# All instructions of an attention and FFN kernel issued in an order that the kernel works out itself

## The chip, the cores and the metric

The kernel runs on one NeuronCore of a Trainium2 chip. The metric is the device time of one execution in microseconds. Five engines run beside each other, each in the order of its own instruction queue: TensorE (PE; its weight loads are listed as PEld), VectorE (DVE), ScalarE (ACT), GpSimd (POOL) and SyncE (SP). SP does nothing here but start DMA transfers, one after another.

## What is computed

The reference is sliding-window attention with a linear bias, followed by a gated FFN. q, k and v have 8 batches, 8 heads, 576 positions and 64 dimensions; the FFN is 512 wide with an inner width of 2048, over 8 x 576 = 4608 rows. All is float32.

```python
scores = scale * np.matmul(q, k.transpose(0, 1, 3, 2))
mask = (rel >= 0) & (rel < 128)                 # rel = query position - key position
scores = np.where(mask, scores - slopes * rel, -1e9)
attn = softmax(scores)                          # slopes: 2 ** -(head + 1)
x = np.matmul(attn, v)                          # then (4608, 512)
h = x @ w_in
g = h * (1.0 / (1.0 + np.exp(-1.702 * h)))
out = g @ w_out
```

## The kernel before

**Number format.** For the large matmuls each float32 operand is split into a rounded high part (type fp32r) and a remainder, and the three products high x high, high x remainder, remainder x high are summed. The weights arrive as 64-bit words and are decoded on the chip: `decode` (L211) runs, for each half megabyte of weights, two ScalarE passes (L219, L220), two VectorE passes (L221, L222), a ScalarE copy that makes the high part (L224) and a GpSimd subtraction that makes the remainder (L225). There are 16 such pieces of w_in and 16 of w_out.

**FFN.** The 4608 rows are cut into 18 chunks of T = 256. A chunk takes 16 steps f. `up(f)` (L448) is twelve matmuls into the tile `h_ps`; then follow the gate, as a Tanh on ScalarE (L457) and a multiplication on VectorE (L458), and the split of g (L461 on ScalarE, L462 on GpSimd). `down(f)` (L465) is six matmuls into two accumulators. A step is thus 18 matmuls, and there are 288 steps. Chunk 0 is done in two parts: its first F0 = 8 steps, then all of chunk 1, then the other 8 of chunk 0. `split_x` (L432) makes the parts of a chunk's input x when the chunk begins.

**Attention.** The work is cut into units of one or two blocks of 128 queries. A unit goes through a software pipeline, one stage per `tick()` (L510): its loads (`load`, `load_v`), the split of q and k, `scores` into `s_ps` (L298), `biased` with the row minimum on VectorE (L314), `exponents` on ScalarE (L328), `normal` (L337), the transposes `flip` into `t_ps` (L351), the copies `high` and `low`, `mix` with v into `x_ps` (L385), and `sum_up`, which writes a part of a chunk's x. Batch 0 is cut into 24 "whole" units: its matmuls are in plain float32, each shown as two in the profile (L303, L393), and its `normal` runs on GpSimd (L345). The other batches use the split format (L309, L398). Chunk 0 can begin when the first 8 units are through.

**What sets the order.** The program is written as one list: an opening of ticks until the first 8 units are mixed, then the 288 steps, with ticks and decodes put between them at a pace worked out from due steps. The framework's own scheduler (`schedule_with_timeline_sim`) then reorders each engine's instructions by its own timeline. Two things are held in the written order: SP's transfers (`move`, L168) and the idle matmuls of `spin` (L193), which keep TensorE busy while it has nothing else: 32 at the start (FIRST_SPINS) and 3 after each tick of the opening. In the opening, weight pair f is fetched four ticks late (`fetch_upto(ticks - FETCH_TICK)`), and the first two decodes are written at ticks 5 and 6.

Tiles come from pools with a number of rotating buffers; a new tile waits until the buffer's last reader is done. `rq` and `rk`, the raw q and k of a unit, have three each, and the table that `tables()` (L177) builds the bias from, `rel`, borrows one of the buffers of `rq`.

Of the kernel before, what the change touches and what calls it, by code (L numbers as in the profile page):

```python
# [21 lines left out]
P = 128  # L22
# [14 lines left out]
BESIDE = range(8, 24)  # L37
FETCH_TICK = 4
DECODE_TICK = 5
# [4 lines left out]
FIRST_SPINS = 32  # L44
SPINS = 3
# [110 lines left out]

@with_exitstack
def tile_kernel(ctx: ExitStack, tc: tile.TileContext, qT, kT, v, w_in, w_out, out):
# [3 lines left out]
    raw = ctx.enter_context(tc.tile_pool(name="raw", bufs=3))  # L162
    att = ctx.enter_context(tc.tile_pool(name="att", bufs=2))
    xp = ctx.enter_context(tc.tile_pool(name="xp", bufs=1))
    ffn = ctx.enter_context(tc.tile_pool(name="ffn", bufs=2))
    ps = ctx.enter_context(tc.tile_pool(name="ps", bufs=1, space=PSUM))

    def move(dst, src):  # L168

        tc.keep_in_program_order(nc.sync.dma_start(dst, src))  # L170
# [6 lines left out]
    def tables():  # L177
# [14 lines left out]

    def spin(n):  # L193

        m = ident.bitcast(BF16)
        for _ in range(n):
            tc.keep_in_program_order(nc.tensor.matmul(idle[:, :2 * P], m[:, :P], m, start=True, stop=True))  # L197
# [4 lines left out]
    def fetch(src, name):  # L202
        st = const.tile([P, 512], I64, name="r" + name, tag=name)
        move(st, src)
        return st
# [5 lines left out]
    def decode(st, name):  # L211

        words = st.bitcast(I32).rearrange("p (m two) -> p m two", two=2)
        top, low = words[..., 1], words[..., 0]
        part = st.bitcast(U16).rearrange("p (m four) -> p m four", four=4)[..., 1]
        bits = ps.tile([P, 4 * P], F32, name="w_ps", tag="t_ps", bufs=2).bitcast(I32)
        w = ffn.tile([P, 512], F32, name="wc", tag="o", bufs=3)

        nc.scalar.activation(bits.bitcast(F32), top.bitcast(F32), AF.Copy, scale=2.0 ** -112)  # L219
        nc.scalar.activation(low, part, AF.Copy, bias=2.0 ** -14 - 0.5, scale=2.0 ** -13)  # L220
        nc.vector.scalar_tensor_tensor(bits, bits, 3, low, ALU.logical_shift_left, ALU.bitwise_or)  # L221
        nc.vector.scalar_tensor_tensor(w.bitcast(I32), top, -0x80000000, bits, ALU.bitwise_and, ALU.bitwise_or)  # L222
        res = const.tile([P, 2, 512], F32R, name=name, tag=name)
        nc.scalar.copy(res[:, 0], w)  # L224
        nc.gpsimd.tensor_tensor(res[:, 1], w, res[:, 0].bitcast(F32), ALU.subtract)  # L225
        return res
# [15 lines left out]
    def load(u):  # L242
# [4 lines left out]
        u.rq = raw.tile([P, 2 * P], F32, name="rq", tag="rq")  # L247
        u.rk = raw.tile([P, 3 * P], F32, name="rk", tag="rk")
        rows = D if u.whole else P
        move(u.rq[:rows, :u.nq], qT[u.pair, :rows, u.q0:u.q0 + u.nq])  # L250
        move(u.rk[:rows, :u.nk], kT[u.pair, :rows, u.k0:u.k0 + u.nk])

    def load_v(u):
        if u.whole:
            u.rv = att.tile([P, 3, D], F32, name="VV", bufs=3)
        else:
            u.rv = raw.tile([P, 3, D], F32, name="rv", bufs=2)
# [3 lines left out]
        if full:  # L261
            move(u.rv[:, :full], v[u.pair, v0:v0 + full * P, :].rearrange("(c p) d -> p c d", p=P))
            u.spans.append((P, slice(0, full)))
        if full < len(u.loaded):
            m = u.loaded[-1].n
            move(u.rv[:m, full], v[u.pair, v0 + full * P:v0 + full * P + m, :])
            u.spans.append((m, slice(full, full + 1)))
        if u.whole:
            for i, c in enumerate(u.loaded):
                c.v = u.rv[:c.n, i]  # L270

    def split_q(u):
# [388 lines left out]
```

## Time and profile before

| | |
|---|---|
| median of 3 runs | 1069.94 us (1067.32 to 1072.7) |
| the profiled execution | 1072.22 us, of which its span is 1070.4 us |
| TensorE matmul, busy | 1054.6 us |
| TensorE weight loads, busy | 941.6 us |
| VectorE / ScalarE / GpSimd, busy | 706.7 / 605.4 / 636.1 us |
| moved by DMA | 81.24 MB, 76 GB/s in the mean |
| mean granted TensorE clock | 0.993 |

The span is the time from the first to the last instruction; the time of the execution is 1.8 us longer. Matmuls overlap in the array, so the duration of one (some 280 ns for 256 columns) is longer than the distance to the next, and a TensorE that is shown as busy need not be at its pace. Its pace is read from the number of matmuls in a stretch, or from the chain of work, where consecutive matmuls stand with the time that they took together.

### The profile page before, as it was taken

How to read it: one execution, taken by the hardware profiler on the slowest of the kernel's cores; microseconds unless marked ns; L12 is line 12 of the kernel's file. 1: busy time of each engine (PE TensorE's matmuls, PEld its weight loads, DVE VectorE, ACT ScalarE, POOL GpSimd, SP SyncE). 2: the span in 40 equal slices, each digit the busy share in tenths (PEclk: the TensorE clock that was granted, in tenths of full speed). 3: DMA queues.
4: the chain of work that ended last, by engine and by line, in shares of the span. 5: the costliest groups of instructions: out<-in, count | busy, mean ns of one | idle time of the engine just before them, and what ended most of it. 6: DMA issues, size and time to landing. Idle time of an engine off the chain costs nothing.

```text
span 1070.4 us, 21794 instructions
## 1 busy us (share of the span) xinstructions
PE 1054.6 (99%) x7021; PEld 941.6 (88%) x7021; DVE 706.7 (66%) x2299; ACT 605.4 (57%) x1797; POOL 636.1 (59%) x931
## 2 busy tenths in 40 slices
PE   7999999999999999999999999999999999999998
PEld 4676899998989999999999999999999999998987
DVE  4767898879897777654676668767867687413131
ACT  4797776676766566444555556656565556322222
POOL 3679986667776666544565657656666566323232
PEclk9799999999999999999999999999999999999999
DMA  4974322333322232202222212222222121000000
GB/s 136 305 235 145 83 63 86 105 84 86 86 79 80 60 88 77 61 12 67 63 71 66 62 52 86 72 69 67 85 67 85 52 68 51 9 12 21 1 21 20
DMA packets 97265, 81.24 MB, mean 76 GB/s; under 512 B 50048, under 2 KB 88448, under 8 KB 97152
## 3 DMA queue, kind: packets, MB, share of 16 engines
q1 hardware_dynamic: 91968, 70.42, 23.4%
q10 hardware_dynamic: 5184, 9.44, 2.4%
q8 instruction: 55, 0.90, 0.3%
q14 instruction: 58, 0.48, 0.1%
HBM read 70.39 MB, written 9.44 MB: 75 GB/s over the span
## 4 chain that ended last, share of the span: by engine, by line
PE 93%; DVE 3%; ACT 2%; DMA 1%; issue 1%; POOL 0%; SPq 0%; DVEq 0%; POOLq 0%; ACTq 0%
PE h_ps L452 37%; PE acc L471 37%; PE x_ps L398 5%; PE t_ps L364 5%; PE s_ps L309 5%; PE s_ps L303 1%; PE x_ps L393 1%; PE acc L197 1%; DMA rk<-kT 1%; DMA rw<-w_in 1%; DVE pb L321 1%; ACT pb L332 0%; ACT rw L220 0%; DVE xh L436 0%; SPq L170 0%
## 5 line engine op out<-in xcount | busy, mean ns | idle before, releaser
L452 PE MATMUL h_ps<-xh,w 128*128 128x256 f32 x2304 | 370.1, 284 | 3.6 <-DVE g L458 2.1
L462 POOL TENSOR_TENSOR gl<-g,gh 128x256 fp32r<-128x256 f32 x288 | 215.7, 750 | 255.8 <-ACT gh L461 194.4
L452 PEld LDWEIGHTS h_ps<-xh,w 128*128 128x128 f32 x2304 | 328.2, 188 | 34.7 <-DVE g L458 3.4
L471 PE MATMUL acc<-w,gh 128*128 128x512 f32 x1152 | 325.5, 399 | 0.0
L458 DVE SCALAR_TENSOR_TENSOR g<-g,h_ps 128x256 f32<-128x256 f32 x288 | 119.4, 415 | 180.5 <-ACT g L457 178.9
L457 ACT ACTIVATE g<-h_ps 128x256 f32<-128x256 f32 x288 | 109.6, 381 | 204.1 <-PE h_ps L452 182.5
L471 PEld LDWEIGHTS acc<-w,gh 128*128 128x128 f32 x1152 | 196.0, 188 | 26.9 <-ACT pw L375 0.6
L461 ACT CAST gh<-g 128x256 fp32r<-128x256 f32 x288 | 116.9, 406 | 141.3 <-DVE g L458 129.3
L452 PE MATMUL h_ps<-xl,w 128*128 128x256 f32 x1152 | 194.6, 280 | 0.0
L471 PE MATMUL acc<-w,gl 128*128 128x512 f32 x576 | 188.1, 401 | 0.0
L332 ACT ACTIVATE pb<-pb,mins 128x256 f32<-128x256 f32 (+3 forms) x292 | 141.4, 486 | 58.7 <-DVE mins L321 55.0
L296 POOL TENSOR_TENSOR K<-rk,K 128x384 fp32r<-128x384 f32 (+1 forms) x140 | 126.8, 906 | 77.7 <-ACT Q L276 22.5
L452 PEld LDWEIGHTS h_ps<-xl,w 128*128 128x128 f32 x1152 | 163.3, 188 | 5.5
L321 DVE CUSTOM_DVE_ANT_0 pb<-s_ps,bias 128x256 f32<-128x256 f32 (+5 forms) x320 | 114.6, 377 | 25.3 <-PE s_ps L303 15.5
L295 POOL TENSOR_TENSOR Q<-rq,Q 64x256 fp32r<-64x256 f32 (+1 forms) x140 | 96.4, 689 | 25.3 <-ACT Q L276 5.7
L349 DVE TENSOR_SCALAR pb<-pb,rec 128x256 f32<-128x256 f32 (+2 forms) x252 | 108.5, 467 | 3.3
L364 PE MATMUL t_ps<-ident,pb 128*128 128x128 f32 (+1 forms) x548 | 100.7, 275 | 1.2 <-DVE pl L381 0.6
L471 PEld LDWEIGHTS acc<-w,gl 128*128 128x128 f32 x576 | 92.4, 188 | 8.2 <-POOL pb L345 0.5
L340 DVE TENSOR_SCALAR rec<-sums 128x2 f32<-128x2 f32 (+2 forms) x164 | 51.1, 312 | 61.3 <-ACT pb L332 60.0
L309 PE MATMUL s_ps<-K,Q 128*128 128x256 f32 (+1 forms) x504 | 91.5, 290 | 0.0
L381 DVE TENSOR_TENSOR pl<-t_ps,ph 128x512 fp32r<-128x512 f32 (+2 forms) x140 | 84.1, 603 | 5.4 <-ACT ph L375 5.1
L294 DVE CAST K<-rk 128x384 fp32r<-128x384 f32 (+1 forms) x140 | 57.5, 411 | 34.2 <-PE s_ps L309 30.2
(56 smaller groups left out, 1277.2 us busy)
## 6 DMA issues: line engine op xcount, KB each, us to landing
rk<-kT SPq DMA_DIRECT2D x84, 192.0 KB, 2.6
rq<-qT SPq DMA_DIRECT2D x112, 128.0 KB, 2.5
out<-o ACTq DMA_DIRECT2D x36, 256.0 KB, 2.3
rw<-w_in SPq DMA_DIRECT2D x16, 512.0 KB, 5.2
rw<-w_out SPq DMA_DIRECT2D x16, 512.0 KB, 6.4
rk<-kT SPq DMA_DIRECT2D x56, 128.0 KB, 2.3
rv<-v SPq DMA_DIRECT2D x100, 64.0 KB, 1.9
rq<-qT SPq DMA_DIRECT2D x44, 64.0 KB, 2.2
```

What stands on the lines that cost most here:

```text
L296: nc.gpsimd.tensor_tensor(K2, rk, K1.bitcast(F32), ALU.subtract)
L309: nc.tensor.matmul(u.s[:b.rows, e, b.first:b.end], u.Q[:, b.q0 - u.q0:b.q0 - u.q0 + b.rows], k[:, ko:ko + b.end - b.first], start=(z == 0) ...
L321: nc.vector.tensor_tensor_reduce(b.p[ra:rb, cs:b.end], u.s[ra:rb, e, cs:b.end], bias[head][ra:rb, cs:b.end], -SCALE, BIG, ALU.add, ALU.min ...
L332: nc.scalar.activation(live, live, AF.Exp, bias=u.mins[:b.rows, e:e + 1], scale=-1.0, accum_out=u.sums[:b.rows, e:e + 1],)
L349: nc.vector.tensor_scalar(live, live, u.rec[:rows, e:e + 1], None, ALU.mult)
L364: nc.tensor.transpose(u.t[:c.n, w:w + b.rows], b.p[:b.rows, col:col + c.n], ident[:b.rows, :b.rows])
L452: nc.tensor.matmul(h, w1[f][:, z, k * P:(k + 1) * P], x[:, k], start=(n == 0), stop=(n == len(ops) - 1))
L457: nc.scalar.activation(g, h, AF.Tanh, scale=0.851)
L458: nc.vector.scalar_tensor_tensor(g, g, 1.0, h, ALU.add, ALU.mult)
L461: nc.scalar.copy(gh, g)
L462: nc.gpsimd.tensor_tensor(gl, g, gh.bitcast(F32), ALU.subtract)
L471: nc.tensor.matmul(acc, g[:, t * P:(t + 1) * P], w2[f][:, z], start=(f == self.f0 and n == 0), stop=(f == self.f1 - 1 and n == 2))
```

## The change

Nothing is added to or taken from the arithmetic. The framework's reordering is switched off (`manual_schedule`). Each helper that used to issue an instruction now records it with `add`: its engine, a time for which it holds the engine (fitted lines such as `62 + 1.055 * n` ns for a VectorE pass over n columns), what it reads and writes, and whether it takes the port that VectorE's fast modes and GpSimd share. At the end `Plan.order()` walks once through time: for each engine it takes the recorded instruction that can start first, and among equals the one written first; a tile takes a free numbered buffer at the moment when its first instruction starts. The instructions are then issued in the order of the starts that this pass found. All matmuls of one third of `up` or of `down` are one entry, as are those of `scores`; a transpose is an entry by itself.

Besides: spins fill the gaps that the pass finds on TensorE in its first 40 us, one for each 213 ns; weight pairs are fetched from the first tick on instead of the fifth; the first two decodes are written at ticks 2 and 3; the high and remainder parts of x are four tiles each instead of one; and `BESIDE` goes, which for units of batch 0 only swapped two stages.

```diff
-BESIDE = range(8, 24)
-FETCH_TICK = 4
-DECODE_TICK = 5
...
-FIRST_SPINS = 32
-SPINS = 3
+READY = {"PE": 1600, "DVE": 4400, "ACT": 2100, "POOL": 2700, "SP": 700}
+HOP = 60
+SPIN = 213
+SPIN_END = 40000
...
+    def order(self):
+
+        free = dict(READY)
...
+                for op in queue[e]:
+                    at = max(op.ready, free[e])
+                    if op.port:
+                        at = max(at, port)
...
+                    if pick is None or (at, op.n) < pick[:2]:
+                        pick = (at, op.n, op)
...
+            for buf in op.opens:
+                free_at = [(0 if s is None else s.done, i) for i, s in enumerate(buf.slots) if s is None or s.left == 0]
+                fits = [x for x in free_at if x[0] <= at]
+                buf.at = max(fits)[1]
...
+            if op.bytes:
+                wire = max(wire, at + op.ns) + op.bytes / 300
+                end = wire + 2000
...
+        done.sort(key=lambda o: o.start)
+        return done
...
+    ctx.enter_context(tc.manual_schedule())
...
+    def pool_two(n):
+        return 140 + 2.17 * n
...
-        rel = raw.tile([P, 2 * P], F32, name="rel", tag="rq")
+        rel = raw.tile([P, 2 * P], F32, name="rel", tag="rq_2")
...
+        add("ACT", lambda: nc.scalar.copy(res.t[:, 0], w.t), 514, r=[w], w=[(res, 0)])
+        add("POOL", lambda: nc.gpsimd.tensor_tensor(res.t[:, 1], w.t, res.t[:, 0].bitcast(F32), ALU.subtract),
+            1254, r=[w, (res, 0)], w=[(res, 1)], port=True)
...
-        xh = xp.tile([P, NC, T], F32R, name="xh")
-        xl = xp.tile([P, NC, T], F32R, name="xl")
+        xh = [buf(xp, [P, T], F32R, f"xh{k}") for k in range(NC)]
+        xl = [buf(xp, [P, T], F32R, f"xl{k}") for k in range(NC)]
...
-    spin(FIRST_SPINS)
     for _ in range(DEPTH):
         load(loads.pop(0))
...
-        spin(SPINS)
-        fetch_upto(ticks - FETCH_TICK)
-        if ticks == DECODE_TICK:
+        fetch_upto(ticks)
+        if ticks == 2:
             w1[0] = decode(w1[0], f"w1_0")
...
+    tables()
+    at = READY["PE"]
+    for op in plan.order():
+        if op.eng == "PE":
+            if op.start < SPIN_END:
+                spin(int((op.start - at) // SPIN))
+            at = op.start + op.ns
+        op.run()
```

**SP at the start.** The rows are transfers, with the number of the tile behind its name and what SP waits for before the row; `rq` and `rk` are a unit's q and k, `VV` its v, `rw` a piece of weights. Before:

```order
L170 DMA rq_137<-qT 64x256
L170 DMA rk_138<-kT 64x256
L170 DMA rq_141<-qT 64x256 [waits DVE_49]
L170 DMA rk_142<-kT 64x256
L170 DMA rq_145<-qT 64x256 [waits DVE_49,Pool_49]
L170 DMA rk_146<-kT 64x256
L170 DMA rq_152<-qT 64x256 [waits DMAHW0_49,PE_49]
L170 DMA rk_153<-kT 64x256 [waits DMAHW1_49]
L170 DMA VV_159<-v 128x2x64
```

and now:

```order
L323 DMA rq_2_107<-qT 64x256 [waits DVE_49,Pool_49]
L323 DMA rk_2_109<-kT 64x256
L323 DMA rq_1_111<-qT 64x256
L323 DMA rk_1_113<-kT 64x256
L323 DMA rq_0_115<-qT 64x256
L323 DMA rk_0_117<-kT 64x256
L323 DMA rq_2_133<-qT 64x256 [waits DMAHW0_49,PE_49]
L323 DMA rk_2_140<-kT 64x256 [waits DMAHW1_49]
L323 DMA rw1_0_0_152<-w_in 128x512
L323 DMA rw2_0_0_155<-w_out 128x512
L323 DMA VV_2_162<-v 128x2x64 [waits DMAHW2_49]
```

The first unit's q now lies in the buffer that `rel` borrows, so that SP's very first transfer, which waited for nothing, waits for VectorE and GpSimd; and the first weights moved from behind the eighth unit's k to behind the fourth's.

**ACT at the first step of the FFN.** L457, now L703, is the first Tanh. L219, L220 and L224 (now L394, L396, L404) are the three ScalarE passes of a decode, `w` the decoded weights with the piece's index behind it, L332 (L539) an exponential, L375 (L597) the copy `high`. Before:

```order
L220 ACTIVATE rw_3_423<-rw_3_423 128x512
L219 ACTIVATE w_ps<-rw_1_334 128x512
L332 ACTIVATE pb,sums<-pb,mins 128x256 x2
L375 COPY pw<-t_ps 128x512
L220 ACTIVATE rw_4_460<-rw_4_460 128x512
L219 ACTIVATE w_ps<-rw_1_336 128x512
L224 CAST w_1_583<-wc 128x512
L219 ACTIVATE w_ps<-rw_2_382 128x512
L220 ACTIVATE rw_4_462<-rw_4_462 128x512
L457 ACTIVATE g<-h_ps 128x256
```

and now:

```order
L404 CAST w_6_0_726<-wc_710 128x512
L396 ACTIVATE rw_7_0_499<-rw_7_0_499 128x512
L597 COPY pw_735<-t_ps_721 128x512
L539 ACTIVATE pb_718,sums_738<-pb_718,mins_719 128x256
L539 ACTIVATE pb_730,sums_738<-pb_730,mins_719 128x256
L404 CAST w_6_0_750<-wc_733 128x512
L394 ACTIVATE w_ps_760<-rw_7_0_483 128x512
L394 ACTIVATE w_ps_774<-rw_7_0_499 128x512
L396 ACTIVATE rw_8_0_545<-rw_8_0_545 128x512
L396 ACTIVATE rw_8_0_552<-rw_8_0_552 128x512
L703 ACTIVATE g_802<-h_ps_762 128x256
```

Where 3 pieces were decoded ahead of the first Tanh (w_1_583 is the third), 14 are now (w_6_0_750 is the fourteenth): eleven decodes moved from behind the FFN's first step to ahead of it.

**PE in the middle.** A stretch in which units and steps alternate. Before:

```order
L398 MATMUL x_ps<-pl,VV 128x256
L471 MATMUL acc_8483<-w_14_1937,gl 128x512
L471 MATMUL acc_8484<-w_14_1937,gl 128x512
L452 MATMUL h_ps<-xh,w_0_296 128x256 x3
L398 MATMUL x_ps<-ph,VV 128x256
L452 MATMUL h_ps<-xh,w_0_296 128x256 x5
L398 MATMUL x_ps<-pl,VV 128x256
L452 MATMUL h_ps<-xl,w_0_296 128x256 x2
L364 MATMUL t_ps<-ident,pb 128x128
L452 MATMUL h_ps<-xl,w_0_296 128x256 x2
```

and now:

```order
L719 MATMUL acc_0_7632<-w_1_0_403,gl_7655 128x512
L719 MATMUL acc_0_7634<-w_1_0_403,gl_7655 128x512
L585 MATMUL t_ps_7693<-ident,pb_6931 128x128
L585 MATMUL t_ps_7693<-ident,pb_7011 128x128 x2
L585 MATMUL t_ps_7693<-ident,pb_7044 128x128
L515 MATMUL s_ps_7700<-K_1_6982,Q_6986 128x256
L515 MATMUL s_ps_7700<-K_1_7038,Q_6986 128x256
L627 MATMUL x_ps_7652<-ph_7629,VV_6929 128x256
L627 MATMUL x_ps_7652<-pl_7645,VV_6929 128x256
L695 MATMUL h_ps_7712<-xh_0_7544,w_3_0_527 128x256
```

The same matmuls now stand in whole groups, where single ones of a unit were put between those of `up`.

More of the change, by code (lines that the diff above doesn't have):

```diff
@@ L43 @@
 SLACK = 2
-FIRST_SPINS = 32
-SPINS = 3
+READY = {"PE": 1600, "DVE": 4400, "ACT": 2100, "POOL": 2700, "SP": 700}
+HOP = 60
+SPIN = 213
+SPIN_END = 40000
+MIXED = ("t", "o")
+ENGINES = ("PE", "ACT", "DVE", "POOL", "SP")
 class Block:
@@ L196, in spin @@
         for _ in range(n):
[L197 removed]
+            nc.tensor.matmul(idle[:, :2 * P], m[:, :P], m, start=True, stop=True)
     w1, w2 = [None] * NF, [None] * NF
     def fetch(src, name):
[L203 to L204 removed]
+        st = buf(const, [P, 512], I64, name, name="r" + name)
+        move(st, src, lambda t: t, 524288, None)
         return st
@@ L211, in decode @@
     def decode(st, name):
[L213 to L225, printed above, removed]
+        def words():
+            w = st.t.bitcast(I32).rearrange("p (m two) -> p m two", two=2)
+            return w[..., 1], w[..., 0]
@@ new lines, in part @@
+        def part():
+            return st.t.bitcast(U16).rearrange("p (m four) -> p m four", four=4)[..., 1]
+        bits = buf(ps, [P, 4 * P], F32, "t", 2, name="w_ps")
+        w = buf(ffn, [P, 512], F32, "o", 3, name="wc")
+        res = buf(const, [P, 2, 512], F32R, name)
+        add("ACT", lambda: nc.scalar.activation(bits.t, words()[0].bitcast(F32), AF.Copy, scale=2.0 ** -112),
+            562, r=[(st, 1)], w=[bits], chain="scale")
+        add("ACT", lambda: nc.scalar.activation(words()[1], part(), AF.Copy, bias=2.0 ** -14 - 0.5, scale=2.0 ** -13),
+            565, w=[(st, 0)], chain="part")
@@ L274, in split_q @@
             return
-        u.Q = att.tile([P, 2 * P], F32R, name="Q")
-        nc.scalar.copy(u.Q[:, :u.nq], u.rq[:, :u.nq])
+        u.Q = buf(att, [P, 2 * P], F32R, "Q", 2)
+        add("ACT", lambda: nc.scalar.copy(u.Q.t[:, :u.nq], u.rq.t[:, :u.nq]), act_cast(u.nq), r=[u.rq], w=[u.Q],
+            chain="split_q")
     def split_v(u):
@@ new lines, in run @@
+        def run():
+            for e, b, qs, ks, zs in runs:
+                to = u.s.t[:b.rows, e, b.first:b.end]
+                if u.whole:
+                    nc.tensor.matmul(to, u.rq.t[:D, qs], u.rk.t[:D, ks], start=True, stop=True)
+                else:
+                    for z, k in enumerate((u.K1, u.K2)):
+                        nc.tensor.matmul(to, u.Q.t[:, qs], k.t[:, ks], start=(z == 0), stop=(z == 1))
+        add("PE", run, ns, 165, r=[u.rq, u.rk] if u.whole else [u.Q, u.K1, u.K2], w=[u.s], chain="scores")
@@ L337, in normal, with run @@
-    def normal(u, on_act):
-        u.rec = att.tile([P, 2], F32, name="rec", bufs=3)
+            def run(e=e, b=b):
+                live = b.p.t[:b.rows, b.live:b.end]
+                nc.scalar.activation(
+                    live, live, AF.Exp, bias=u.mins.t[:b.rows, e:e + 1], scale=-1.0,
+                    accum_out=u.sums.t[:b.rows, e:e + 1])
+            add("ACT", run, 300 + 0.8 * (b.end - b.live), 95, r=[u.mins], w=[b.p, (u.sums, e)], chain="exp")
+    def normal(u, on_act=False):
+        u.rec = buf(att, [P, 2], F32, "rec", 3)
@@ L374, in high @@
         for m, a, z in u.pspans:
-            nc.scalar.copy(u.ph[:m, a:z], u.t[:m, a:z])
+            add("ACT", lambda m=m, a=a, z=z: nc.scalar.copy(u.ph.t[:m, a:z], u.t.t[:m, a:z]), act_psum(z - a),
+                r=[u.t], w=[(u.ph, a)], chain="high")
     def low(u):
```

431 lines of the change are left out of this document (302 added, 129 removed).

## The prediction

> **What bounds the kernel now.** I read the page's first lines, then busy time and the number of matmuls by stretches, then the chain of waits for the distance between matmuls.
>
> ```profile
> span 1070.4 us, 21794 instructions
> ...
> PE 1054.6 (99%) x7021; PEld 941.6 (88%) x7021; DVE 706.7 (66%) x2299; ACT 605.4 (57%) x1797; POOL 636.1 (59%) x931
> ```
>
> TensorE is shown busy for all but 16 us, so there seems to be nothing to win. The stretches say more: the opening up to the first full step of `up` (0 to 45), the stretch in which the weights are still being decoded (to 153), the middle, and the end, where almost only the FFN is left.
>
> ```profile
> core 0: us, PE busy (x) PEld busy (x) DVE busy (x) ACT busy (x) POOL busy (x), PEclk, DMA share, GB/s
> 0.00:45.00 45.00, 39.08 (x176) 24.11 (x176) 22.60 (x93) 23.79 (x68) 21.46 (x33) 0.85 0.65 193
> ...
> 45.00:153.00 108.00, 104.12 (x642) 83.00 (x642) 85.68 (x255) 90.43 (x242) 94.04 (x108) 1.00 0.51 155
> 153.00:910.00 757.00, 755.06 (x5204) 693.71 (x5203) 558.21 (x1861) 445.97 (x1374) 473.77 (x727) 1.00 0.25 71
> 910.00:1066.00 156.00, 156.00 (x1004) 140.76 (x1002) 38.94 (x92) 45.24 (x115) 46.85 (x64) 1.00 0.03 11
> ```
>
> From 45 to 153 ScalarE (84%) and GpSimd (87%) are nearly full; in the middle no engine but TensorE is above 74%. The Trainium skill (Perfetto Trace Analysis, Identifying the Most-Contended Engine) calls matmul busy time a poor measure of TensorE and the busy share of the weight loads a good one. The trace agrees that the two differ: weight loads fill 83.00 of 108 us, 77%, in the second stretch and 140.76 of 156, 90%, in the last.
>
> What each stretch would take at TensorE's own pace comes from counts and distances. Counts, by tile in the same stretches (`h_ps` and `acc` three rows each, then `s_ps`, `t_ps`, `x_ps` two each, from 45 on):
>
> ```profile
> 45.00:153.00 108.00, 42.09 (x285) 37.15 (x285) 9.41 (x23) 9.02 (x24) 1.00 0.51 155
> 153.00:910.00 757.00, 375.21 (x2520) 344.29 (x2520) 86.83 (x210) 79.50 (x210) 1.00 0.25 71
> 910.00:1066.00 156.00, 90.30 (x649) 87.21 (x648) 23.12 (x55) 21.11 (x55) 1.00 0.03 11
> ...
> 45.00:153.00 108.00, 38.87 (x135) 1.00 0.51 155
> 153.00:910.00 757.00, 363.62 (x1260) 1.00 0.25 71
> 910.00:1066.00 156.00, 91.44 (x336) 1.00 0.03 11
> ...
> 45.00:153.00 108.00, 13.68 (x61) 1.00 0.51 155
> 153.00:910.00 757.00, 86.64 (x476) 1.00 0.25 71
> ...
> 45.00:153.00 108.00, 9.93 (x61) 1.00 0.51 155
> 153.00:910.00 757.00, 83.06 (x452) 1.00 0.25 71
> ...
> 45.00:153.00 108.00, 16.55 (x100) 1.00 0.51 155
> 153.00:910.00 757.00, 84.52 (x496) 1.00 0.25 71
> ```
>
> Distances, from the chain (start, time, what, how many):
>
> ```profile
> 62.55 1.06 PE s_ps L303 x4
> ...
> 65.67 1.01 PE x_ps L393 x6
> ...
> 683.93 0.44 PE t_ps L364 x4
> 684.37 0.47 PE s_ps L309 x4
> ...
> 685.89 0.35 PE x_ps L398 x3
> ...
> 686.70 1.41 PE h_ps L452 x12
> ...
> 711.59 1.40 PE acc L471 x6
> ```
>
> So `h_ps` is 0.1175 us apart, `acc` 0.233, `t_ps` 0.11, split `s_ps` and `x_ps` 0.117, plain float32 `s_ps` 0.265 and `x_ps` 0.168.
>
> - 45 to 153: 285 x 0.1175 + 135 x 0.233 + 61 x 0.11 = 71.7. Of the 61 `s_ps`, 32 are plain (half of them for the narrow last units, counted at 0.2 by their columns) and 29 split: 7.4 + 3.4. Of the 100 `x_ps`, 80 are plain (48 at 0.168, 32 narrow ones, counted at 0.11) and 20 split: 11.6 + 2.3. Sum 96.4; **11.6 us are lost**.
> - Middle: 296.1 + 293.6 + 49.7 + 55.7 + 58.0 = 753.1, some 5 less since about a tenth of the `s_ps` and `x_ps` are half as wide: **4 to 9 us are lost** of 757.
> - End: 649 x 0.1175 + 336 x 0.233 and some 2 us of attention are 156.5 of 156: nothing is lost.
>
> **The change part by part.** The arithmetic is the same, so all that can change is the opening and the 16 to 21 us above.
>
> *SP's start.* What follows are VectorE's bias tables, SP's first transfer, the 32 spins, the first scores, two stretches of DMA, and a median time to landing.
>
> ```profile
> 2.88 1.50 DVE L191 TENSOR_SCALAR bias<-rel 128x256 bf16<-128x256 f32 x7
> ...
> 0.74 0.57 SPq L170 DMA_DIRECT2D rq<-qT  x1
> ...
> 1.62 6.33 PE L197 MATMUL acc<-ident 128*128 128x256 bf16 x32 [1.62 <-POOL ident masks.py:199]
> 7.87 0.92 PE L303 MATMUL s_ps<-rk,rq 64*128 64x128 f32 x4
> ...
> 23.00:38.00 15.00, 12.87 (x40) 7.65 (x40) 8.78 (x26) 9.85 (x25) 7.01 (x8) 0.54 0.89 267
> 38.00:45.00 7.00, 6.84 (x35) 4.33 (x34) 4.60 (x21) 6.00 (x17) 4.48 (x5) 1.00 0.97 310
> ...
> rk<-kT SPq DMA_DIRECT2D x84, 192.0 KB, 2.6
> ```
>
> Now SP's first transfer waits for the tables, which end at 2.88 + 1.50 = 4.4 instead of starting at 0.7. Its second, the first k, is issued at 5.0 and lands some 2.2 to 2.6 later, so the first scores come at about 7.4. Before, 32 spins held them until 7.87; now 11 spins (at 6.33 / 32 = 0.2 us each) are through at 3.8. The two cancel: gain 0.4.
>
> *Weights ahead of the units.* In the new order 18 weight pieces and the loads of 12 units, 11.8 MB, stand in SP's queue up to the v that the last `mix` ahead of the first `h_ps` reads. At the 310 GB/s of a full queue that is 38 us, at the 267 of the stretch in which SP also waited for buffers 44. From 4.4 on, and with 2.6 to land, the first `up` starts at 45 or 51. I take 45.5, for the queue now always holds weights to send: 0.5 later than now. By then 9 units are mixed and 13 scored, instead of 8 and 12, which is 1.01 + 1.06 = 2.1 us less for later.
>
> *Decodes ahead of the FFN.* ScalarE's prices, by the distance of starts:
>
> ```profile
> 45.69 0.62 ACT L224 CAST w<-wc 128x512 fp32r<-128x512 f32 x1
> 46.20 0.64 ACT L219 ACTIVATE w_ps<-rw 128x512 f32<-128x512 f32 x1
> 46.77 0.69 ACT L220 ACTIVATE rw<-rw 128x512 int32<-128x512 uint16 x1
> 47.35 0.37 ACT L457 ACTIVATE g<-h_ps 128x256 f32<-128x256 f32 x1
> ...
> L332 ACT ACTIVATE pb<-pb,mins 128x256 f32<-128x256 f32 (+3 forms) x292 | 141.4, 486 | 58.7 <-DVE mins L321 55.0
> ```
>
> A decode costs ScalarE 0.51 + 0.57 + 0.58 = 1.66 us, so the eleven that move take 18 us out of the 90 that it works between 45 and 153: from 84% to 67%, the level of the middle, where 0.5 to 1.2% is lost. They don't come free. Ahead of the first Tanh stand 14 + 16 + 18 passes of decodes, 24 exponentials and 10 copies: 7.1 + 9.1 + 10.4 + 24 x 0.49 + 10 x 0.4 = 42 us (a copy of 384 columns estimated at 0.4, from the Tanh's 0.37 for 256). Starting after the first scores, at 8.5, with no pause, ScalarE reaches the first Tanh at 50.5 (47.35 now), and a pause of a few us while the first weights land is likely. TensorE, with two `up`, a `mix` and scores in hand (2 x 1.41 + 2.1), runs out at 50.4 and waits some 3 us. So the loss of this stretch goes from 11.6 to 3 + 2 = 5, the 2 being the middle's rate on 96 us and as much again. Bounds: 1 (the middle's rate alone) and 11.6 (nothing won).
>
> *The middle.* Its order is regrouped, not shortened. Of the 4 to 9 lost I take 2.5 off, half of what lies between; bounds a gain of 9 (all of it) and a loss of 11, at 0.1 us for each of its 113 units (452 transposes, four to a unit). The split of `xh` and `xl` into four tiles and the swap of `normal` and `high` go with this; the busiest helper there, VectorE at 74%, covers them.
>
> *The end.* Nothing to win; its last `down` waits for the same chain as now. 0.
>
> Sum: +0.5 - 0.4 - 2.1 - 6.6 - 2.5 = -11.1. The profiled execution took 1072.2 (its span 1070.4 and 1.8 around it), 2.3 above the median of 1069.9; 1072.2 - 11.1 - 2.3 = **1059 us**. By the weight loads, as the Trainium skill has it, the loss from 45 to 153 would be 108 - 83.00 / 0.902 = 16 us, and the sum 4 lower, 1055.
>
> **Rivals.** *The opening comes later.* At 267 GB/s the first `up` starts at 51.5. Against it, the queue is fuller; for it, SP also waits for buffers of units in that queue. 1059 + 6 = 1065.
>
> *TensorE at half its clock, slower than before.* At 3.8 the 11 spins are through and no data is there before 7.4. The trace has the clock at 0.54 from 23 to 38, so at half for some 14 of those 15 us, although TensorE worked for 12.87 of them.
>
> ```profile
> 26.46 0.82 PE L197 MATMUL acc<-ident 128*128 128x256 bf16 x3
> ...
> 28.28 1.65 PE L303 MATMUL s_ps<-rk,rq 64*128 64x128 f32 x4 [0.15 <-DVE mins L321]
> ```
>
> At that clock scores take 1.65 instead of 0.92 and a spin 0.27. A unit's matmuls (0.92 scores, 0.33 transposes, some 0.9 for its mix) become 1.8 times as long, 3.9 us, and with 83 spins over 9 units (9 x 0.27) 6.3 us: 9 x 6.3 + 7.4 = 64 and a first `up` 18 us late, 1077. It decides from 5.2 us a unit on, where the gain of 11 is gone. Against it: such a row of work leaves no pause, and DMA sets the pace. The Trainium skill (TensorE: Matmul & The Clock Gate, What's actually happening) has the clock fall after an idle window of about 3.4 us and return after about 3.4 us of sustained work. The fall agrees with the trace in kind; the return took some 14 us there. By that rule the case would end within one or two units and cost 3 us.
>
> *The order doesn't help.* The pass foresees each duration by a line in n; where one is late, all behind it on its engine wait, and nothing reorders. At 0.1 us for each of the 113 units of the middle the gain is gone: 1070. Against it, the slack of all helpers there.
>
> *All losses go.* Opening at 42, loss 1 from 45 to 153, none in the middle: 1059 - 3.5 - 4 - 4 = 1047.
>
> **How the numbers follow.** Forecast 0.52 (1052 to 1066 by its bounds), later opening 0.15, half clock 0.09, no help 0.12, all losses 0.12. A measurement of this kernel tells 0.5%, 5.3 us, from no change, so faster means below 1064.6: nine tenths of the forecast, two fifths of the later opening, all of the last: 0.65. Slower, above 1075.3: most of the half clock and a little of no help, 0.10. Within: 0.25. The range reaches from the last case to no help: 1047 to 1071.
>
> **What would show it.** First transfer at 4.4; first full `up` near 45 and the first Tanh after 50; granted clock 1 from 10 to 45; weight loads above 85% in the 100 us after the first step, GpSimd and ScalarE below 80%; the middle at 2520 `h_ps` in 750 to 757 us; the end unchanged. I am wrong if the first `up` lies beyond 52, if the clock stays at half in the opening, or if the middle takes over 760 for those 2520.

## The result and the profile after

The changed kernel took 1101.63 us in the median of four runs (1100.58 to 1105.79), the kernel before 1071.32 beside it (1067.32 to 1073.13): 1.0295 times as long, 95% interval 1.0254 to 1.0337. The prediction was 1059, with a range of 1047 to 1071.

The page's first lines, the busy times, and the shares of the chain that ended last, by engine:

```profile
span 1098.8 us, 22127 instructions
...
PE 1067.5 (97%) x7050; PEld 942.6 (86%) x7050; DVE 697.5 (63%) x2299; ACT 621.1 (57%) x1797; POOL 638.7 (58%) x931
...
PE 85%; DVE 8%; ACT 3%; issue 2%; POOL 1%; DMA 0%; ACTq 0%; DVEq 0%; SPq 0%; POOLq 0%
```

and the same shares before:

```profile
PE 93%; DVE 3%; ACT 2%; DMA 1%; issue 1%; POOL 0%; SPq 0%; DVEq 0%; POOLq 0%; ACTq 0%
```

The profiled execution took 1100.58 us. VectorE now holds 8% of the chain that ended last, where it held 3%, although its own busy time is 9 us lower than before. So the same work is waited for more often.

Where the time went is read from the Tanh, one for each of the 288 steps. The lines give shortest, median and longest duration, then the start of the first and of the last, before and after:

```profile
L457 ACT ACTIVATE g<-h_ps x288: 358/384/425, 47.4 to 1062.3; 128x256 f32<-128x256 f32 x144
```
```profile
L703 ACT ACTIVATE g<-h_ps x288: 376/384/397, 58.4 to 1091.4; 128x256 f32<-128x256 f32 x144
```

| start of the Tanh, us | before | after | later by |
|---|---|---|---|
| first | 47.4 | 58.4 | 11.0 |
| 25th (all weights decoded) | 159.1 | 170.4 | 11.3 |
| last | 1062.3 | 1091.4 | 29.1 |

The opening costs 11 us, the next 111 us nothing either way, and the rest, which the prediction had 2.5 us faster, 17.8. TensorE's waits from the 25th step on (line that waits, line waited for, us in all, times, longest), first before, then after:

```profile
PE t_ps L364 <- DVE pl L381: 0.6, 1, 0.6
PE t_ps L364 <- DVE pb L349: 0.6, 2, 0.3
PE h_ps L452 <- DVE g L458: 0.5, 1, 0.5
```
```profile
PE h_ps L695 <- DVE xh L675: 5.4, 5, 1.1
PE h_ps L695 <- DVE g L704: 2.8, 5, 1.0
PE x_ps L627 <- DVE xf L666: 1.4, 2, 1.2
PE acc L719 <- ACT gh L706: 1.0, 3, 0.4
```

New are five waits of some 1.1 us for `xh`, the cast of x that `split_x` makes when a chunk begins. One of them in the order of time (start, length, engine, line; in brackets the idle time and what ended it), before and after:

```profile
758.19 1.71 DVE L436 CAST xh<-xf 128x256 fp32r<-128x256 f32 x4
...
758.88 0.87 POOL L462 TENSOR_TENSOR gl<-g,gh 128x256 fp32r<-128x256 f32 x1
```
```profile
779.19 0.29 DVE L675 CAST xh<-xf 128x256 fp32r<-128x256 f32 x1
...
779.76 0.46 POOL L471 TENSOR_TENSOR VV<-rv,VV 128x128 fp32r<-128x128 f32 x1
...
780.30 0.46 POOL L485 TENSOR_TENSOR Q<-rq,Q 64x128 fp32r<-64x128 f32 x1
...
780.84 0.73 POOL L488 TENSOR_TENSOR K<-rk,K 128x256 fp32r<-128x256 f32 x1
...
781.09 1.46 DVE L675 CAST xh<-xf 128x256 fp32r<-128x256 f32 x2
...
782.47 0.96 DVE L677 TENSOR_TENSOR xl<-xf,xh 128x256 fp32r<-128x256 f32 x1
...
783.35 0.81 DVE L675 CAST xh<-xf 128x256 fp32r<-128x256 f32 x1
...
784.22 0.86 PE L695 MATMUL h_ps<-xh,w 128*128 128x256 f32 x5 [1.13 <-DVE xh L675]
```

Before, the four casts stood together and were done 1.7 us after the first began. Now they take 5.0 us: behind the first cast the pass put three GpSimd operations, since it never lets a cast (`port=True`) and a GpSimd operation overlap, and the casts that come later meet GpSimd all the same and take 0.7 to 0.8 us instead of 0.29. In the pass's own times the four are done 2.7 us after the first begins, so it did not foresee the other 2.3.

### The profile page after: what moved, and what is told of

Read it like the earlier page. It is cut to its first block, busy times and chain, and to the rows that moved or that the text cites. A ratio compares the mean times of both kernels' runs of the same rounds, so it can differ in the third digit from the quotient of the medians.

```text
span 1098.8 us, 22127 instructions
## 1 busy us (share of the span) xinstructions
PE 1067.5 (97%) x7050; PEld 942.6 (86%) x7050; DVE 697.5 (63%) x2299; ACT 621.1 (57%) x1797; POOL 638.7 (58%) x931
## 4 chain that ended last, share of the span: by engine, by line
PE 85%; DVE 8%; ACT 3%; issue 2%; POOL 1%; DMA 0%; ACTq 0%; DVEq 0%; SPq 0%; POOLq 0%
PE h_ps L695 34%; PE acc L719 33%; PE t_ps L585 5%; PE s_ps L515 5%; PE x_ps L627 5%; DVE xh L675 2%; PE s_ps L512 1%; DVE xl L677 1%; PE x_ps L621 1%; DVE g L704 1%; DVE xf L666 1%; DVE pb L527 1%; DVE pb L562 1%; ACT pb L539 0%; DVE wc L401 0%
## 5 line engine op out<-in xcount | busy, mean ns | idle before, releaser
L695 PE MATMUL h_ps<-xh,w 128*128 128x256 f32 x2304 | 328.4, 284 | 9.6 <-DVE xh L675 5.4
L695 PEld LDWEIGHTS h_ps<-xh,w 128*128 128x128 f32 x2304 | 301.8, 189 | 27.5 <-DVE g L704 9.5
L719 PE MATMUL acc<-w,gh 128*128 128x512 f32 x1152 | 317.2, 396 | 1.1 <-ACT gh L706 1.0
L704 DVE SCALAR_TENSOR_TENSOR g<-g,h_ps 128x256 f32<-128x256 f32 x288 | 120.8, 419 | 222.3 <-ACT g L703 216.6
L703 ACT ACTIVATE g<-h_ps 128x256 f32<-128x256 f32 x288 | 110.7, 384 | 242.2 <-PE h_ps L695 227.5
L695 PE MATMUL h_ps<-xl,w 128*128 128x256 f32 x1152 | 184.6, 282 | 0.0
L719 PE MATMUL acc<-w,gl 128*128 128x512 f32 x576 | 180.7, 395 | 0.0
L539 ACT ACTIVATE pb<-pb,mins 128x256 f32<-128x256 f32 (+3 forms) x292 | 141.3, 485 | 40.3 <-DVE mins L527 27.9
L719 PEld LDWEIGHTS acc<-w,gl 128*128 128x128 f32 x576 | 107.2, 187 | 27.4 <-POOL gl L707 1.4
L562 DVE TENSOR_SCALAR pb<-pb,rec 128x256 f32<-128x256 f32 (+2 forms) x252 | 114.1, 487 | 3.1
L585 PE MATMUL t_ps<-ident,pb 128*128 128x128 f32 (+1 forms) x548 | 93.8, 276 | 8.9 <-DVE wc L401 5.9
L585 PEld LDWEIGHTS t_ps<-ident,pb 128*128 128x128 f32 (+1 forms) x548 | 68.7, 141 | 36.2 <-POOL pb L558 10.9
L597 ACT CAST ph<-t_ps 128x512 fp32r<-128x512 f32 (+2 forms) x140 | 72.8, 520 | 33.0 <-PE t_ps L585 31.7
```

The source lines that it names most:

```text
L539: nc.scalar.activation(live, live, AF.Exp, bias=u.mins.t[:b.rows, e:e + 1], scale=-1.0, accum_out=u.sums.t[:b.rows, e:e + 1])
L562: nc.vector.tensor_scalar(live, live, rec, None, ALU.mult)
L585: nc.tensor.transpose(u.t.t[:c.n, w:w + b.rows], b.p.t[:b.rows, col:col + c.n], ident[:b.rows, :b.rows])
L695: nc.tensor.matmul(h.t, w.t[:, z, k * P:(k + 1) * P], x[k].t, start=(part == 0 and k == 0), stop=(part == 2 and k == NC - 1))
L703: add("ACT", lambda: nc.scalar.activation(g.t, h.t, AF.Tanh, scale=0.851), act_psum(T), r=[h], w=[g])
L704: add("DVE", lambda: nc.vector.scalar_tensor_tensor(g.t, g.t, 1.0, h.t, ALU.add, ALU.mult), dve_one(T), r=[h], w=[g])
```

## The experiments

Behind each time stand, in brackets, its ratio to the kernel before, run beside it, and the 95% interval of that ratio. The median of the kernel before was 1071.0 to 1073.4 us in these sittings, so two experiments can differ by some 2 us for no reason of theirs.

**Casts ahead of the rest.** A lower number for the operations of `split_x`:

```diff
-            add("DVE", lambda k=k: nc.vector.tensor_copy(xh[k].t, x.t[:, k]), 205, r=[(x, k)], w=[xh[k]], port=True)
+            add("DVE", lambda k=k: nc.vector.tensor_copy(xh[k].t, x.t[:, k]), 205, r=[(x, k)], w=[xh[k]], port=True, shift=-100)
...
-                335 if k % 2 else 697, r=[(x, k), xh[k]], w=[xl[k]], port=True)
+                335 if k % 2 else 697, r=[(x, k), xh[k]], w=[xl[k]], port=True, shift=-100)
```

> The changed kernel with one thing altered: the eight operations that split x at a chunk's start are given a number lower by 100, so that the pass lets them ahead of GpSimd's work for later units at the shared port. Theory (boundary): at five chunk starts TensorE waits 1.05 to 1.13 us for the last cast of xh, and 0.46 us once more 5.7 us later, together about 9 us; with the casts first these waits go, the time falls by 6 to 9 us to about 1094, and the groups of h_ps show a wait for the casts below 2 us in all. Rival (a fixed order only moves its waits): what is passed over waits instead (transposes for the softmax, or the sums of x), and the time stays within 3 us of 1101.6.

1109.25 us (1.035, 1.0301 to 1.04): slower still, by more than the 3 us that the rival allowed. The waits for `xh` are nearly gone, but others took their place:

```profile
PE x_ps L627 <- DVE xf L666: 5.8, 6, 1.2
PE h_ps L695 <- DVE g L704: 5.7, 9, 0.7
PE h_ps L695 <- DVE xh L675: 0.4, 1, 0.4
```

The rival's mechanism was right here: casts that pass in front of the sums of x (L666) and the gate (L704) hold those up. (Some 1.5 us of the 7.6 more belong to another effect, the place of tiles, which comes below.)

**Weights later.** Fetch and first decodes at the ticks of the kernel before:

```diff
-        fetch_upto(ticks)
-        if ticks == 2:
+        fetch_upto(ticks - 4)
+        if ticks == 5:
             w1[0] = decode(w1[0], f"w1_0")
-        if ticks == 3:
+        if ticks == 6:
```

> The changed kernel, but the weights are fetched and the first two decoded as late in the opening as in the kernel before (four steps later). Theory (opening): the 11 us by which the first Tanh came later (58.4 against 47.4) are the price of weight pieces in SP's queue ahead of units and of decodes ahead of the units' own steps on ScalarE, VectorE and GpSimd; with both later the first Tanh is at 46 to 50, and the total falls by 8 to 11 us to about 1092. Rival 1 (the fixed order costs the opening by itself, by SP's late start and the missing reordering): first Tanh at 55 or later, total within 3 us of 1101.6. Rival 2 (work moved behind the first Tanh comes back there): first Tanh early, but by the 24th the lead is below 4 us.

1104.0 us (1.0292, 1.0238 to 1.0346), first Tanh at 59.6. That looks like the first rival, but a second thing had changed. From 8 to 46 us TensorE shows no idle time, and yet does 112 matmuls in 38 us, and the spins in it are 0.21 us apart until 45 (8 in 1.89), 0.11 from 47.6 on (10 in 1.26):

```profile
8.00:46.00 38.00, 38.00 (x112) 18.86 (x112) 13.94 (x65) 15.92 (x48) 13.41 (x18) 1.00 0.58 177
```
```profile
41.85 1.89 PE L367 MATMUL idle<-ident 128*128 128x256 bf16 x8
...
47.60 1.26 PE L367 MATMUL idle<-ident 128*128 128x256 bf16 x10
```

TensorE ran at half its clock, with DMA at 58%. (The clock column reads 1.00 there: the first record of the clock in this trace comes at 46.4, and the column is 1.00 ahead of it.) In the changed kernel itself the first record is at 20.4, and the same four scores take 1.58 us ahead of it and 0.85 behind it:

```profile
16.22 1.58 PE s_ps L512 x4
...
18.20 0.64 PE idle L367 x3
...
20.97 0.85 PE s_ps L512 x4
```

So the clock had to be held up before the weights could be judged.

**More spins.** 32 ahead of the first scores, as before the change, with early and with late weights:

```diff
     tables()
+    spin(21)
     at = READY["PE"]
```

> The changed kernel with 21 idle matmuls more ahead of the first scores, 32 as in the kernel before; nothing else. The changed kernel's records show spins 0.213 us apart until 20.4 us and 0.109 from then on, so TensorE ran at half its clock until then; in the kernel before full clock came at 7.1. Theory (clock): with 32 spins full clock comes at 7 again, the 6 to 7 us of work that ran at half from 8 to 20 take half, and the first Tanh comes 2 to 4 us earlier, total 1097 to 1099. Rival (from 23 us on ScalarE and the decodes set the pace, whatever TensorE does): full clock at 7, but the first Tanh moves by less than 1 us and the total stays within 2 us of 1101.6.

> The changed kernel with the weights fetched and the first two decoded four steps later, as in the kernel before, and with 32 spins ahead of the first scores. With later weights alone TensorE stayed at half clock until 46.4 us, and the first Tanh came at 59.6. Theory (weights and decodes ahead of the units cost the opening): with the clock back the first Tanh comes at 45 to 50, the total at 1088 to 1093. Rival (the fixed order itself holds the opening up): first Tanh at 54 or later, total 1098 or more.

Full clock now came at 4.8 and 6.7 us. With early weights: first Tanh at 55.8, 1100.72 us (1.0275, 1.0246 to 1.0304); in this trace the clock fell to half again from 45.7 to 56.0, behind 3.4 us in which TensorE was busy for 1.75, and the total is the same within its spread. With late weights the clock stayed full: first Tanh at 44.3, 1089.14 us (1.0167, 1.0147 to 1.0187), 12.5 less than the changed kernel. So the same 21 spins bring the first Tanh 2.6 us earlier behind early weights and 15.3 behind late ones (59.6 to 44.3): each of the two costs hides the other. First Tanh, early and late weights:

```profile
L703 ACT ACTIVATE g<-h_ps x288: 377/386/391, 55.8 to 1090.4; 128x256 f32<-128x256 f32 x144
```
```profile
L703 ACT ACTIVATE g<-h_ps x288: 364/385/391, 44.3 to 1079.5; 128x256 f32<-128x256 f32 x144
```

**Transfers or decodes?** Early weights and 32 spins, but every decode from the ninth on waits in the pass for the first chunk's casts:

```diff
+                held[0] = last_cast if halves >= 8 else None
                 ws[g] = decode(ws[g], f"w{1 + halves % 2}_{g}")
```

> The changed kernel with 32 spins, weights fetched as early as it does, but all decodes from the ninth on held in the pass until the first four casts to xh, so that 8 decodes lie ahead of the first Tanh (as with later weights) instead of 16. Tells decodes from transfers: with 16 decodes and 21 weight pieces landed the first Tanh came at 55.8, with 8 and 12 at 44.3. Theory (the decodes cost the opening): first Tanh at 45 to 49. Rival (the transfers of weights ahead of the units' data cost it): 52 or later.

```profile
L707 ACT ACTIVATE g<-h_ps x288: 378/386/389, 52.2 to 1100.4; 128x256 f32<-128x256 f32 x144
```

52.2: the rival, if narrowly. Taken in this order, of the 14.1 us between 58.4 and 44.3 the spins are 2.6 (58.4 to 55.8), eight decodes fewer 3.6 (to 52.2), and the early weight pieces 7.9 (to 44.3). By the landing times of the trace the v of the ninth unit, whose mix is the last ahead of the first `up` in the changed kernel, landed at 52.6 there, at 49.7 with the decodes held, at 40.2 with late weights, and at 42.7 in the kernel before. Part of the 7.9 comes by way of the clock: with the decodes held it was at half again from 45.3 to 52.1, and TensorE was busy for all of these 6.8 us, so that may have cost up to 3.4 (an estimate: half of it). In all 1109.56 us in two runs (1.0329, 1.0266 to 1.0392): the decodes held back are missing later, and from the 7th to the 9th Tanh 29.6 us pass instead of 17.0.

**Early weights under the automatic ordering.** One part of the change put into the kernel before:

```diff
-FETCH_TICK = 4
-DECODE_TICK = 5
+FETCH_TICK = 0
+DECODE_TICK = 2
```

> The kernel before, with its automatic ordering, but the weights fetched from the first step on and the first two decoded at steps 2 and 3, as the changed kernel has it: one part of the change alone. Theory (opening): early weights cost the opening under any ordering: first Tanh 6 to 11 us later, total 1077 to 1082. Rival (only the fixed order cannot fit the decodes between the units' steps): first Tanh within 2 us of 47.4 and the total within 3 us of 1071, or up to 6 us faster, as the prediction had it.

1088.17 us (1.0156, 1.0106 to 1.0206), 17 more, where the theory's 1077 to 1082 are 6 to 11 more. First Tanh at 54.6 (7.2 later, as it said), the 25th 15.4 later, and from the 65th to the last the lag only goes from 14.9 to 17.7. So the early weights harm under either ordering, and nearly all of their harm lies ahead of the 80th step; most of the 17.8 us that the changed kernel loses behind its 25th step has to come from the new order.

**Tables in other buffers.** `rel` and `rel_i` in the buffers `rq_0` and `rq_1`, so that SP's first transfer does not wait.

> The changed kernel, but the two work tiles of the bias tables stand in the buffers that the second and third unit load into, so SP's first transfer does not wait for the tables. Expected by the theory that transfers pace the opening from the start: first transfer at 0.7 instead of 4.7, first scores 3 to 4 us earlier, first Tanh 3 to 4 us earlier, total about 1098. Rival (from 16 us on ScalarE and the decodes pace the opening, and start no earlier): scores come earlier, the first Tanh by less than 1.5 us, total within 1.5 us of 1101.6.

First transfer at 0.7 and first scores at 3.8 instead of 7.6, first Tanh at 57.5 instead of 58.4, 1098.89 us (1.025, 1.0193 to 1.0308). The rival in the opening; of the 3.8 us 0.9 arrived. The median lies 2.7 us lower, nearer to the theory's 1098, but the two profiled executions took 1100.95 and 1100.58, so no gain in the total is shown. In this trace the clock was at half from 48.1 to 58.4, which may have taken some of what came earlier.

**Casts without the port rule.**

```diff
-            add("DVE", lambda k=k: nc.vector.tensor_copy(xh[k].t, x.t[:, k]), 205, r=[(x, k)], w=[xh[k]], port=True)
+            add("DVE", lambda k=k: nc.vector.tensor_copy(xh[k].t, x.t[:, k]), 205, r=[(x, k)], w=[xh[k]])
```

> The changed kernel, but the pass no longer keeps the four casts to xh (VectorE) apart from GpSimd's operations at the shared port; order among VectorE's operations otherwise by the same rules. In the changed kernel these casts spread over 4.9 us at the chunk starts with attention (1.9 us at the others), against 1.7 us in the kernel before, where single casts take 0.82 us beside GpSimd too. Theory (the port rule lets the casts wait behind each GpSimd operation): spread falls to 2 to 3 us, the five waits of 1.05 to 1.13 us for xh and those of 0.46 after them go, total 6 to 9 us less, about 1094. Rival (contention at the port is real, and casts beside GpSimd all take 0.8 us): spread stays above 3 us, the waits stay or move to the operations behind, total within 3 us of 1101.6.

1091.73 us (1.019, 1.0171 to 1.021), 9.9 less, a little beyond the theory's range; in the traces 6.7 of it lie behind the 25th Tanh (from there to the last 914.3 us instead of 920.9). The four casts take 3.6 us instead of 5.0 at the chunk starts with attention, not the 2 to 3 of the theory (single ones still take up to 0.9 us), and 1.6 instead of 1.9 at the others. The waits for them are gone, and five shorter ones for the softmax's scaling came:

```profile
PE t_ps L585 <- DVE pb L562: 3.4, 5, 0.7
PE s_ps L515 <- DVE mins L527: 1.2, 2, 0.9
PE h_ps L695 <- DVE g L704: 1.0, 1, 1.0
```

**All three.** Later weights, 32 spins, free casts:

> Later weights, 32 spins and free casts together. If the opening costs 9 to 11 us by the weights and the clock, and the chunk starts 6 to 9 us by the casts, the two add up: 1080 to 1086. If the waits only move from one place to the next, 1092 or more.

1065.83 us (1065.55 to 1066.01), 0.9944 of the kernel before, interval 0.9925 to 0.9964: 0.6% faster than the kernel before, and far below the 1080 that was expected. But 35.8 us less than the changed kernel is 13 more than 12.5 + 9.9, and the waits do not explain it: they are those of the kernel with free casts (3.8, 0.9 and 1.2 us for the same three lines). What differs is the distance between matmuls that wait for nothing, here twelve `h_ps` of one step, in the kernel with late weights and spins and then in this one:

```profile
565.47 1.43 PE h_ps L695 x12
```
```profile
561.28 1.38 PE h_ps L695 x12
```

**The place of a tile.** Over all undisturbed neighbours between 200 and 1040 us (h_ps to h_ps under 140 ns, acc to acc under 260) the mean distance is nearly the same in some kernels with different orders, and differs by up to 4 ns between others. What goes with it is where x and g lie in the on-chip memory of the built program. Below, a place is the address of their tiles less that of the first weight tile, modulo 256 bytes; all tiles of x and g, with their high and remainder parts, have the same one in a kernel. Small tiles ahead of them, whose number and order follow the order of the instructions, move all that lies behind by steps of 32. Five kernels move them and leave every engine's instructions and their order as they were:

```diff
-buf(att, [D, P], F32, "carry", 1)
+buf(att, [D, P + 24], F32, "carry", 1)     # 96 bytes; P + 8: 32; P + 16: 64
...
-u.mins = buf(att, [P, 2], F32, "mins", 3)
+u.mins = buf(tail, [P, 2], F32, "mins", 3) # a pool behind all others
```

The longer `carry` pushes x and g up; `mins` behind all others lets them down by 96 bytes in the kernel before and by 64 in the changed one, where 32 more of `carry` make it 32.

> The changed kernel with one tile (carry) 96 bytes longer and nothing else: no instruction is added or moved, only the tiles of x, g and their halves lie 96 bytes further on. Theory (place in memory): in eight runs the mean distance between two h_ps matmuls goes with the address of the x and g tiles modulo 128, weights lying at 0: 119.2 ns at 0, 117.1 at 32, 115.5 at 64, 118.35 at 96 (the changed kernel); with them at 64 it falls to 115.5 and that of acc from 232.8 to 230.1, 3456 x 2.8 + 1728 x 2.7 = 14.5 us, total about 1087. Rival (the distances differ by the order of the instructions, the address is a coincidence): distances stay at 118.3 and 232.8, total within 2 us of 1101.6.

> Later weights, 32 spins and free casts as in the run of that name, with the tile 64 bytes longer, which brings x and g from 64 back to 0 modulo 128. Theory (place in memory): h_ps from 115.5 to 119.2 ns, acc from 230.1 to 232.1, 3456 x 3.7 + 1728 x 2 = 16 us more: 1082, which would also explain why the three edits together gave 13 us more than one by one. Rival (the edits help each other): total within 2 us of 1065.8.

> The kernel before with the same tile 32 bytes longer, which brings x and g from 32 to 64 modulo 128. Theory (place in memory): h_ps from 117.1 to 115.5 ns, acc from 233.1 to 230.1: 3456 x 1.6 + 1728 x 3 = 10.7 us less, 1061. Rival: no change beyond 2 us from 1071.5.

> The kernel before, with the three 8-byte tiles mins in a pool of their own behind all others; no instruction added. x and g move down by 96 bytes, from 32 to -64 modulo 256 against the weights. Theory (place): h_ps from 117.1 to 115.5 ns, acc from 233.1 to 230.1, 3456 x 1.6 + 1728 x 3 = 10.7 us less, 1061. Rival (115.5 belonged to that kernel's order): distances unchanged, total within 2 us of 1071.5.

> The changed kernel, mins in a pool of their own and carry 32 bytes longer, so that x and g lie at -64 instead of -32; no instruction added. Theory (place): h_ps from 118.35 to 115.5 ns, acc from 232.8 to 230.1, 14.5 us less, 1087. Rival: within 2 us of 1101.6.

| place | kernels (median us) | h_ps, ns | acc, ns |
|---|---|---|---|
| -64 | all three (1065.83), changed kernel moved (1093.34) | 115.5, 115.5 | 230.1, 229.9 |
| -64 | before, moved (1067.7) | 116.2 | 231.7 |
| -32 | changed kernel (1101.63) | 118.35 | 232.8 |
| 0 | later weights + spins (1089.14), all three + 64 bytes (1077.45) | 119.3, 119.2 | 232.2, 232.2 |
| 32 | before (1071.32) | 117.1 | 233.1 |
| 64 | changed kernel + 96 (1101.39), before + 32 (1071.85) | 117.35, 117.5 | 233.4, 232.9 |

The expectations for the first and third counted modulo 128 and missed: 96 and 32 bytes led to 64, not to -64. The one that took the fastest kernel to 0 came with the distances foretold (119.2 and 232.2) and cost 11.6 us of the 16 worked out. The two that put both kernels at -64 bear the place out. In the changed kernel the distances are those foretold (115.5 and 229.9); from the 25th to the last Tanh it takes 910.9 us instead of 920.9, and the median falls by 8.3 of 14.5, since its opening was 3.5 us later this time, with the clock at half until 25.9. The kernel before came closer to the place's distances, to 116.2 and 231.7, but not all the way (its `h_ps` stand more singly, which may be why), and to 0.9962 of its time (0.994 to 0.9984), 1067.7 instead of the 1061 worked out. The other nine kernels of this document stand at -64, -32, 0 or 32, and their distances are within some 0.2 ns of the table's. So at one place, -64, the mended fixed order takes 0.9944 and the automatic one 0.9962 of the kernel before, with intervals that overlap: no gain of the fixed order over the automatic one is shown. Twelve `h_ps` in the fastest kernel at 0 and in the changed kernel at -64:

```profile
560.03 1.43 PE h_ps L695 x12
```
```profile
564.68 1.38 PE h_ps L696 x12
```

**Two last ones.** The softmax's scaling without the port rule too, and more spins for the kernel before:

> Later weights, 32 spins, free casts, and VectorE's scaling of the softmax (L562) also no longer kept apart from GpSimd in the pass. In the run without this, TensorE waited 0.73 to 0.81 us for that scaling at five chunk starts. Theory (the port rule delays it as it did the casts): these waits go, 3 to 4 us less, 1062. Rival (the port itself delays it): within 1.5 us of 1065.8.

> As before_moved, with 8 spins instead of 3 after each step of the opening. In the kernel before the granted clock was at half from 24.2 to 37.8 us; with later weights and more spins in the fixed order it stayed full and the first Tanh came at 44.3 instead of 47.4. Theory (the pauses let the clock fall, and the half clock costs 3 us): clock full through the opening, first Tanh 2 to 3 us earlier than in before_moved. Rival (transfers pace the opening at that point): first Tanh within 0.5 us, or later by the spins' own time.

The first took 1085.63 us (1.0118, 1.009 to 1.0147), 20 more than without the edit. Its place is the same, -64. The five waits for L562 are gone, but the waits of over 0.1 us, counted from start to start, went from some 9 to some 24 us in all, spread over 55 places; the largest in the waits view:

```profile
PE h_ps L695 <- DVE g L704: 4.0, 4, 1.9
PE x_ps L627 <- DVE xf L666: 2.8, 10, 1.3
PE acc L719 <- DVE o L740: 2.8, 4, 0.7
PE s_ps L515 <- DVE mins L527: 1.5, 2, 1.3
```

So neither "no rule" nor "always the rule" is right. The second took 1071.07 us: it kept the clock full to 90 us and brought the first Tanh from 45.3 to 43.7, less than the theory's 2 to 3 us, but the time to 0.9987 (0.9969 to 1.0005), no better than without the added spins.

## Why the prediction was wrong

Two steps of the sum failed. The first `up`, taken at 45.5, came at 55.6, and the middle, taken as a gain of 2.5 us, was a loss of 17.8. A third, the 6.6 us to win while the weights are decoded, did not come. All three signs that the prediction named for itself being wrong were there: the first `up` beyond 52, half clock in the opening, and 774 us for the 2520 `h_ps` behind 153.

- **SP's start.** First transfer foreseen at 4.4, scores at 7.4; they came at 4.7 and 7.6. What the step left out of the sum was the clock: the 32 spins had brought full clock at 7.1, and without 21 of them it came at 20.4. The rival of half clock named this and priced it at 18 us with a chance of 0.09 (the pace at which it takes up the gain is 5.5 us a unit by its own sum, not 5.2). In the changed kernel it was worth 2.6 us at the first Tanh, and in the total no more than the runs scatter; behind late weights it was worth 15.3.
- **Weights ahead of the units.** The first `up` at 45.5 was the step that failed first. It let the queue run at 310 GB/s from its first transfer on. In the trace it ran at 211 from 4.7 to 23, half clock among the reasons (with 32 spins the ninth v landed at 48.8 instead of 52.6), and at 299 from there to 52.6. Ahead of that v stood 18 weight pieces, where the kernel before had 10, and it landed 9.9 us later than before. Moving the weights back gave 7.9 us of the first Tanh. The later opening that I gave as a rival, 51.5, was also too early.
- **Decodes ahead of the FFN.** "They don't come free" was priced at 3 us, most of it a guessed pause of ScalarE (its passes end at 50.5, TensorE runs out at 50.4), and the eight held back in the experiment cost 3.6. But the gain set against it, 6.6 us, was no gain: the 11.6 us "lost" between 45 and 153 were mostly not waits, for TensorE is shown idle for 3.9 of these 108 us. The stretch from the first to the 25th Tanh took 111.7 us before and 112.1 after, although ScalarE's load in it fell from 82% (91.30 of 112 us) to 69% (76.88). A part of a gain can be hidden in this: the clock of the changed kernel was at half from 102.3 to 109.2, with TensorE busy for 5.5 us of it, so up to 2.8 us by estimate. What the rest of the 11.6 is, no run tells.
- **The middle.** Taken as -2.5 with a bound of +11, it was +17.8 from the 25th to the last Tanh. Waits are counted here from start to start, as what a distance between two matmuls has beyond the usual one of its kind; that is a little more than the idle time that the waits view shows. Those of over 0.1 us grew by some 12 us (4 to 16), and 12.0 of the 16 stand at chunk starts: 6.2 for `xh`, 3.7 for the gate, four of these five waits 5.7 us behind one for `xh`, and eight of 0.26 in the chunk starts without attention. "The busiest helper there, VectorE at 74%, covers them" was read from a mean; the burst at the chunk start is what decides, and the pass foresaw it as 2.7 us where it took 5.0. Free casts took back 6.7 of these us, and 9.9 in the whole run. Another 3.4 are the place: 3168 `h_ps` at 1.2 ns more, 1584 `acc` at 0.3 less. Behind most waits the second matmul came 0.1 us late as well (22 times, 10 before), 1.3 us more. Some 1 us is left unexplained.
- **The end.** "Unchanged" fell too: the last 31 steps took 1.3 us more. One wait of 0.26 at the chunk start among them and some 0.4 for the place are about half of it; the other half is open.
- **The rival "the order doesn't help"** had the mechanism, a foreseen duration that is missed and nothing that reorders, but at 0.1 us for each unit everywhere. It struck at few places, some ten times as hard. The pass's own starts of the first and the last Tanh are 49.8 and 1047.7; the chip's were 58.4 and 1091.4.

The opening (11.0), the stretch to the 25th Tanh (0.3), and behind it the waits (some 12), the place (3.4) and the rest (some 2.4) make the 29.1 us by which the last Tanh is later.

## What to carry to other kernels

A fixed order is as good as its worst-foreseen burst: look at the places where one tile is waited for by all that follows (here a chunk's start), compare how long its makers take from first to last in both traces, and do not judge cover by mean busy shares. When an edit is meant to remove lost time, first show that the time is waits, by the waits view, and not what the instructions cost anyway. And before crediting a 1% gain or loss to an order, compare the distance between matmuls that wait for nothing: if it moved, look where the tiles lie. An opening with two causes of delay can hide either of them: here late weights showed nothing until the clock was held up.

## What the runs showed of the hardware

- **Place.** The mean distance of two matmuls at full clock was 115.4 to 119.3 ns for one and the same shape (128x128 weights, 256 columns), and 229.9 to 233.4 for 512 columns, by where x and g lay. Between the places -64 (115.5) and 0 (119.2) the difference comes to 13 us in 3456 `h_ps` and 4 in 1728 `acc`, and 11.6 us were measured. It held over kernels of different orders; why it is so, no run here tells. Only five places, 32 bytes apart, were tried, and the weights lay at one address in all kernels: whether the distance from the weights or the address of x and g decides, and whether 256 bytes is the period, is not shown (128 is not: -64 and 64 differ). The Trainium skill (SBUF — State Buffer, SBUF: two separate sides) says that TensorE waits on no other engine in this memory, and that only the port shared by VectorE and GpSimd causes contention, as a lock for the whole instruction. The casts agree with the lock (0.29 us alone, 0.7 to 0.8 beside GpSimd).
- **Clock.** Changes of the granted clock lie a whole number of 3.41 us apart (full from 20.42 for 81.92 us, 24 of them, in the changed kernel). It can stay at half for 38 us in which TensorE shows no idle time (plain float32 scores and mixes, transposes and few spins, 8 to 46 us). The Trainium skill (TensorE: Matmul & The Clock Gate, What's actually happening) has it return after one window of some 3.4 us of sustained work; the spacing agrees, the return does not, so work that the profile shows as busy is not always enough for it. No run here isolated which of these instructions fails to count.
